# A gated mix of attention and MLP: the first attention turn put into the MLP's last token tile, and the MLP in text order

## The chip, the core and the metric

The kernel runs on one core of a Trainium2 chip. The time is the device time of one execution in microseconds (us); lower is better. The core's engines are named as the profile names them: PE (TensorE, matmuls; PEld is its weight load), DVE (VectorE), ACT (ScalarE), POOL (GpSimd) and SP (SyncE, which here only issues DMAs). PE writes into PSUM, which has eight banks of 128 x 512 fp32 numbers. The profile also shows the clock that PE was granted, 1.00 being full speed.

## The reference

x has 2048 tokens of 448 features, all in fp32:

```
a = attention(x)                 # 16 heads of 28: softmax(q k^T / sqrt(28)) v, then @ wo
b = gelu(layernorm(x) @ w1 + b1) @ w2 + b2      # 448 -> 1792 -> 448
g = sigmoid(sum(x * gate_w))     # one number for each token
out = g * a + (1 - g) * b
```

The kernel reaches fp32 accuracy by splitting each operand of the large products into a high and a low part (`..h`, `..l`) and adding three products: high x high, high x low, low x high. To split means a rounding copy on ACT and a subtraction on DVE or POOL. The 448 features lie in four rows of 128 partitions, of which the last holds high and low halves of the remaining 64, so a product over the features is 11 matmuls and not 12.

## The kernel before

**Stages.** Tokens go in four chunks c of 512, each of four token tiles of 128.

1. *Projections.* For each chunk seven `qk_tile` (11 matmuls each, L161) and four `v_tile` (L175), results stored to DRAM. Layer norm's statistics are made beside them: `ln_stats(i)` (L194) fetches two token tiles of x and takes batch-norm statistics and aggregates on DVE, `ln_rows` (L201) makes rows of mean and 1/std, and `ln_turn(a, b)` (L207) turns them so that they lie along the tokens: for mean and for 1/std a transpose on PE into one bank, a copy on DVE, a DMA to DRAM. The first turn stands in chunk 1, the second in chunk 3. `ln_load` (L105) fetches the rows of a chunk back, to all partitions; `ln_fetch` (L110) and `ln_apply` (L114) make the normed input y of a chunk.
2. *MLP.* For each chunk, `mlp1(f)` for 14 groups f of 128 hidden features (11 matmuls, L451; ACT makes gelu twice, rounded L454 and full L455; POOL makes the low part hl, L456), then `mlp2(c, i)` for four token tiles (14 x 3 matmuls, L463 to L466; ACT copies the result, L469; SP stores it to gbs, L470). In chunk 0 the weights are loaded and split on the way: `load_w1` (L87: DMA, ACT copy, POOL subtraction), three f ahead, and `load_w2` (L96: DMA, ACT copy, DVE subtraction), through a staging tile with three buffers.
3. *Attention.* Units of work are the 512 queries of one head against 128 keys. A turn takes U = 5 units: `scores` (L620) makes 15 products (L629) into banks 0 to 4, with the exponentials of three units in one ACT instruction and of two in another (L634); then `pv_mm` (L655) multiplies earlier turns' exponentials by v into bank 7. There are 205 turns.

**Fillers.** The exponentials need each query's largest score. `RowMax` (L262) gets these: a matmul of queries by keys (L321) into a bank, then a reduce on DVE (L301 one bank, L303 two banks at once). There are 1040 such pieces, 65 for each group of 4 heads and chunk of queries, the 65th being `close` (L285: a transpose, a negated copy, a DMA to `ms`). They fill in between other work: 476 of them (MLP_MAX) in the MLP, where `Filler.run` (L370) lets a group of six go into banks 2 to 7 each time that enough have come due over the slots of the MLP's matmuls; the others in attention, up to three for each turn, in banks 5, 6 and 5. `load_qm(n)` (L424) brings the maxima of a chunk of queries into the query tile, and before that forces whatever pieces are still missing for it, one by one through bank 5.

**Order.** PE takes its matmuls in the order of the program text in all stages. On the other engines the order of the projections and the MLP is worked out by a scheduler, that of attention is the text's. An engine with its order fixed can only do its next instruction: where that waits, all behind it wait too.

**Between the MLP and attention.** After mlp1 of chunk 3, the first keys, queries and values are fetched. Turn 0 follows the last token tile. At its start SP issues the loads of `khi(1)` and of b2 (`b2b`, L679), and for k = 2 to 5 `load_wo` (L590: DMA, then DVE's cast woh at L593, then POOL's subtraction). The gate's sigmoid (L611 to L614) stands ahead of turn 0. The last turns project the results (`finish`, `gated`, `finish_last`).

```
         for i in range(TPC):
             if c + 1 < NC:
                 ln_fetch(c + 1, i)
                 ln_apply(c + 1, i)
             mlp2(c, i)
```

## Time and profile before

| | |
|---|---|
| runs | 1151.25, 1142.76, 1155.83 us; median 1151.25 |
| profiled execution | 1146.98 us; span 1145.2 us, mean granted clock 0.991 |
| projections | 0 to 126.7 us of the span |
| MLP | 126.7 to 486.4 us |
| attention | 486.4 us to the end |
| DVE, largest group | reduces of row maxima (L301), 624 of 687 ns, 413.4 us |
| ACT, largest group | exponentials (L634), 410 of 1234 ns, 484.6 us |

The page gives for each engine its busy time, share of the span and number of instructions. Its second part cuts the span into 40 equal slices of 28.6 us, one digit each: the busy tenths, or for PEclk the granted clock in tenths. A timeline row gives start, duration, engine, line, operation, what is written and read, shape, and in brackets how long the engine was idle before it and what ended that.

### The profile page before, as it was taken

The page shows a single profiled execution, that of the slowest core. Times are in us where ns is not written, and L with a number is a line of the kernel's source. Part 1 is how long each engine was busy: PE and PEld are TensorE (multiplying, and loading weights), DVE is VectorE, ACT ScalarE, POOL GpSimd, SP SyncE. Part 2 cuts the span into 40 slices and gives each one's busy share as a digit, 9 for nine tenths or more (in the row PEclk, how much of TensorE's full clock was granted, in tenths as well). Part 3 has the DMA queues.
Part 4 walks back from the last instruction along what each step waited for, and adds up shares of the span by engine and source line. Part 5 has one row for each costly group of instructions (what it writes and reads, how often), then busy time and mean ns, then how long its engine had stood idle before and what let it go on. Part 6 is the DMA issues. An engine that isn't in the chain of part 4 may idle for free.

```text
span 1145.2 us, 19823 instructions
## 1 busy us (share of the span) xinstructions
PE 1116.6 (98%) x8136; PEld 678.4 (59%) x8136; DVE 731.6 (64%) x1033; ACT 635.9 (56%) x668; POOL 331.0 (29%) x355
## 2 busy tenths in 40 slices
PE   6999989999999999989999999999999999999998
PEld 4778867777767777744444444444444444454556
DVE  3433287888878888666676766676676667646103
ACT  5324551132033032067887878878787887848463
POOL 4043367146044032011123012311222123444250
PEclk9999999999999999989999999999999999999999
DMA  8878643002100014062101211111121003002201
GB/s 269 277 217 303 208 141 88 25 9 68 47 23 18 25 30 114 25 168 72 30 12 36 52 40 40 36 27 39 31 64 36 18 19 91 12 25 68 66 26 49
DMA packets 53519, 84.35 MB, mean 74 GB/s; under 512 B 8676, under 2 KB 28660, under 8 KB 52628
## 3 DMA queue, kind: packets, MB, share of 16 engines
q1 hardware_dynamic: 49236, 76.96, 22.5%
q0 software_dynamic: 4192, 6.12, 2.1%
q8 instruction: 64, 1.05, 0.4%
q14 instruction: 27, 0.22, 0.1%
HBM read 56.40 MB, written 26.49 MB: 72 GB/s over the span
## 4 chain that ended last, share of the span: by engine, by line
PE 89%; DMA 4%; POOL 3%; DVE 2%; issue 1%; ACT 1%; SPq 0%; POOLq 0%; ACTq 0%; DVEq 0%
PE bank L658 22%; PE bank L629 20%; PE bank L321 15%; PE bank L451 10%; PE bank L168 4%; PE bank L466 4%; PE bank L463 4%; PE bank L464 4%; PE bank L184 2%; PE bank L525 1%; DMA bxr<-in_xk 1%; PE bank L526 1%; PE bank L527 1%; DMA xraw<-in_xt 1%; POOL hl L456 1%
## 5 line engine op out<-in xcount | busy, mean ns | idle before, releaser
L634 ACT ACTIVATE pt<-bank 128x1536 f32<-128x1536 f32 (+1 forms) x410 | 484.6, 1234 | 155.9 <-PE bank L629 155.9
L301 DVE TENSOR_REDUCE mx<-bank 128x1 f32<-128x512 f32 x624 | 413.4, 687 | 174.9 <-PE bank L321 161.0
L658 PE MATMUL bank<-pt,vg 128*32 128x512 f32 x2048 | 263.7, 606 | 0.0
L303 DVE TENSOR_REDUCE mx<-bank 128x2 f32<-128x1024 f32 x200 | 235.4, 1219 | 41.1 <-PE bank L321 41.0
L321 PE MATMUL bank<-khi,qd 28*128 28x512 f32 x512 | 241.6, 479 | 0.3 <-DVE mx L301 0.2
L321 PEld LDWEIGHTS bank<-khi,qd 28*128 28x128 f32 x512 | 92.3, 181 | 148.3 <-DVE mx L301 107.0
L629 PE MATMUL bank<-qh,klo 28*128 28x512 f32 x1024 | 179.0, 395 | 0.0
L629 PE MATMUL bank<-qh,khi 29*128 29x512 f32 x768 | 161.8, 484 | 0.3 <-ACT h L469 0.3
L451 PE MATMUL bank<-y,w1f 128*128 128x512 f32 x616 | 153.2, 400 | 0.6 <-ACT h L455 0.6
L451 PEld LDWEIGHTS bank<-y,w1f 128*128 128x128 f32 x616 | 113.8, 190 | 36.1 <-issue 12.5
L629 PE MATMUL bank<-ql,khi 28*128 28x512 f32 x768 | 133.6, 393 | 0.0
L456 POOL TENSOR_TENSOR hl<-h,hh 128x512 fp32r<-128x512 f32 x56 | 72.5, 1295 | 172.0 <-ACT h L455 160.8
L658 PEld LDWEIGHTS bank<-pt,vg 128*32 128x32 f32 x2048 | 45.7, 108 | 84.6 <-issue 83.1
L629 PEld LDWEIGHTS bank<-qh,klo 28*128 28x128 f32 x1024 | 90.2, 186 | 4.2
L321 PE MATMUL bank<-khr,qd 28*128 28x512 f32 x512 | 80.7, 467 | 7.3 <-DVE mx L303 4.2
L541 POOL DMA_DIRECT2D lt<-ob x15 | 10.8, 723 | 265.7 <-DVE ob L540 265.7
L466 PE MATMUL bank<-w2h,hl 128*128 128x448 f32 x224 | 85.1, 380 | 1.9 <-POOL hl L456 1.9
L469 ACT ACTIVATE h<-bank 128x448 f32<-128x448 f32 x16 | 8.7, 543 | 140.4 <-PE bank L466 140.4
L629 PEld LDWEIGHTS bank<-qh,khi 29*128 29x128 f32 x768 | 63.3, 183 | 36.8 <-ACT pt L634 32.1
L463 PE MATMUL bank<-w2h,hh 128*128 128x448 f32 x224 | 84.7, 378 | 0.3 <-ACT hh L454 0.3
L454 ACT ACTIVATE hh<-bank,b1s 128x512 fp32r<-128x512 f32 x56 | 38.4, 685 | 81.9 <-PE bank L451 81.8
L464 PE MATMUL bank<-w2l,hh 128*128 128x448 f32 x224 | 82.3, 368 | 0.0
(100 smaller groups left out, 1237.0 us busy)
## 6 DMA issues: line engine op xcount, KB each, us to landing
qk<-hl SPq DMA_DIRECT2D x28, 512.0 KB
xraw<-in_xt SPq DMA_DIRECT2D x16, 256.0 KB
vs<-vt SPq DMA_DIRECT2D x16, 256.0 KB
r<-in_xt SPq DMA_DIRECT2D x16, 256.0 KB
rc<-rls POOLq DMA_DIRECT2D x60, 64.0 KB, 2.2
bxr<-in_xk SPq DMA_DIRECT2D x8, 448.0 KB
r<-in_w SPq DMA_DIRECT2D x14, 256.0 KB
gbs<-h SPq DMA_DIRECT2D x16, 224.0 KB
```

Source lines behind the costliest of these rows:

```text
L168: nc.tensor.matmul(ps, a, b, start=(i == 0), stop=(i == len(ops) - 1))
L301: nc.vector.reduce_max(self.mx[:, c0:c0 + 1], bank[:, b0], axis=AX)
L303: nc.vector.reduce_max(self.mx[:, c0:c1 + 1:c1 - c0], bank[:, b0:b1 + 1], axis=AX)
L321: nc.tensor.matmul(bank[:, b], self.qds[self.n][r, i * P:(i + 1) * P], khi[self.n // NC][r, k * 512:(k + 1) * 512], start=True, stop=True)
L451: nc.tensor.matmul(ps, a, b, start=(i == 0), stop=(i == len(ops) - 1))
L456: nc.gpsimd.tensor_sub(hl[f], h, hh[f].bitcast(F32))
L463: nc.tensor.matmul(a, hh[f][:, sl], w2h[f], start=(f == 0), stop=False)
L464: nc.tensor.matmul(a, hh[f][:, sl], w2l[f], start=False, stop=False)
L466: nc.tensor.matmul(a, hl[f][:, sl], w2h[f], start=False, stop=(f == NF - 1))
L629: nc.tensor.matmul(bank[:, u % U], a[r, k * P:(k + 1) * P], b[r], start=(i == 0), stop=(i == 2))
L634: nc.scalar.activation(t, bank[:, b:b + len(units)], AF.Exp, scale=SCALE)
L658: nc.tensor.matmul(pv[32 * j:32 * j + 32, :], vg[n // NC][:, k, 32 * j:32 * j + 32], probs.pop(4 * step + j), start=(k == 0), stop=(k == N ...
```

## The change

Three things are changed.

1. *Layer norm's statistics.* The fetch of x (`stats_fetch`) and its use (`ln_stats`) are two functions, called at different tiles, the use two tiles or so after the fetch. In `ln_turn` both transposes come first, and one copy moves both rows; the first turn is one tile later, and `ln_load(0)`, `ln_fetch(0, ..)` and `ln_apply(0, ..)` are moved with it.
2. *The MLP in text order* on SP, POOL, ACT and DVE too. Weights are fetched (`fetch_w1`, `fetch_w2`) and split (`split_w1`, `split_w2`) apart: in chunk 0, step f fetches w1 of f+3 and w2 of f, runs mlp1(f), then splits w1 of f+2 and w2 of f-1. Staging is two tiles used in turn, and during the weights' loading the two halves of `lnr` as well. A chunk's `ln_apply` comes behind the token tile's matmuls, not ahead of them.
3. *The first turn of attention* (units 0 to 4) stands within the last token tile's matmuls, after its group f = 4. That tile accumulates in bank 7 and takes no fillers, so 476 pieces are spread over 42 slots fewer. The turn's exponentials go into a tile each of `klo` and `vg`. The gate's operations come ahead of chunk 3's token tiles. In attention the loop skips `scores` for turn 0, and with it the call that asks how many fillers are due.

The diff, cut:

```diff
-    def staged(width):
-        return my.tile([P, CH], F32, name="r", bufs=3)[:, :width]
+    stages, turn = [my.tile([P, CH], F32, name=f"s{i}") for i in range(2)], 0
+
+    def staged(width=CH):
+        nonlocal turn
+        turn += 1
+        return stages[turn % len(stages)][:, :width]
...
+    def split_w1(f):
+        r = wraw.pop((1, f)).rearrange("p (t x) -> p t x", t=4)
         t = mw1.tile([P, 8, P], F32R, name=f"w1f{f}")
         w1h[f], w1l[f] = t[:, 0:4], t[:, 4:8]
-        r = r.rearrange("p (t x) -> p t x", t=4)
         nc.scalar.activation(w1h[f], r, AF.Copy)
         nc.gpsimd.tensor_sub(w1l[f], r, w1h[f].bitcast(F32))
...
+    def split_w2(f):
+        r = wraw.pop((2, f))
         nc.scalar.activation(w2h[f], r, AF.Copy)
         nc.vector.tensor_sub(w2l[f], r, w2h[f].bitcast(F32))
...
             for n in range(2):
-                r = qw.tile([b - a, P], F32, name=f"rows{a}{n}")
                 nc.tensor.transpose(ps[:b - a, n * P:(n + 1) * P], mr[:, n, a:b], ident)
-                nc.vector.tensor_copy(r, ps[:b - a, n * P:(n + 1) * P])
-                nc.sync.dma_start(lns[n * NT + a:n * NT + b], r)
+            r = qw.tile([b - a, 2, P], F32, name=f"rows{a}")
+            nc.vector.tensor_copy(r, ps[:b - a, :2 * P].rearrange("p (n i) -> p n i", n=2))
+            for n in range(2):
+                nc.sync.dma_start(lns[n * NT + a:n * NT + b], r[:, n])
...
-                if c == 1 and m == 1:
+                if c == 1 and m in (1, 2):
+                    ln_stats(m - 1)
+                if c == 1 and m == 3:
                     ln_rows(0, TPC)
-                if c == 1 and m == 5:
+                if c == 1 and m == 6:
                     ln_turn(0, TPC)
...
+                if c == 3 and m == 1:
+                    stages += [lnr[:, 0], lnr[:, 1]]
...
     def mlp2(c, i):
 
         sl = slice(i * P, (i + 1) * P)
-        a = bank[:, i % 2, :D]
+        last = c * TPC + i == NT - 1
+        a = bank[:, 7 if last else i % 2, :D]
...
-            filler.run(1)
+            if not last:
+                filler.run(1)
+            elif f == NF // 3:
+                scores(list(range(U)), 0, early)
...
+    with tc.manual_schedule(engines={E.SP, E.Pool, E.Activation, E.DVE}):
+        for c in range(NC):
+            for f in range(NF):
+                if c == 0:
+                    if f + 3 < NF:
+                        fetch_w1(f + 3)
+                    fetch_w2(f)
...
+                    if f == FS:
+                        filler.spread(nc.sync, MLP_MAX, (NC * NF - FS) * 23 - 3 * NF)
+                mlp1(f)
+                if c == 0:
+                    if f + 2 < NF:
+                        split_w1(f + 2)
+                    if f > 0:
+                        split_w2(f - 1)
...
+                nc.scalar.activation(gate, zall, AF.Exp, scale=-1.0)
...
+            for i in range(TPC):
+                mlp2(c, i)
+                if c + 1 < NC and i < 3:
+                    ln_apply(c + 1, i)
...
-            scores(units, min(3, filler.due()))
+            if u:
+                scores(units, min(3, filler.due()), lambda n: ap.tile([P, n, CH], F32, name=f"pt{n}"))
```

More of the change, by code (lines that the diff above doesn't have):

```diff
@@ L82, with fetch_w1, fetch_w2 @@
     w1h, w1l, w2h, w2l = {}, {}, {}, {}
-    def staged(width):
-        return my.tile([P, CH], F32, name="r", bufs=3)[:, :width]
-    def load_w1(f):
-        r = staged(CH)
-        nc.sync.dma_start(r, w1[f].rearrange("p t x -> p (t x)"))
+    stages, turn = [my.tile([P, CH], F32, name=f"s{i}") for i in range(2)], 0
[3 more added lines that the diff above has]
+        return stages[turn % len(stages)][:, :width]
+    wraw = {}
+    def fetch_w1(f):
+        wraw[1, f] = staged()
+        nc.sync.dma_start(wraw[1, f], w1[f].rearrange("p t x -> p (t x)"))
+    def split_w1(f):
+        r = wraw.pop((1, f)).rearrange("p (t x) -> p t x", t=4)
         t = mw1.tile([P, 8, P], F32R, name=f"w1f{f}")
         w1h[f], w1l[f] = t[:, 0:4], t[:, 4:8]
-        r = r.rearrange("p (t x) -> p t x", t=4)
         nc.scalar.activation(w1h[f], r, AF.Copy)
         nc.gpsimd.tensor_sub(w1l[f], r, w1h[f].bitcast(F32))
-    def load_w2(f):
-        r = staged(D)
-        nc.sync.dma_start(r, w2[f])
+    def fetch_w2(f):
+        wraw[2, f] = staged(D)
+        nc.sync.dma_start(wraw[2, f], w2[f])
+    def split_w2(f):
+        r = wraw.pop((2, f))
         nc.scalar.activation(w2h[f], r, AF.Copy)
@@ L110, in ln_fetch @@
     def ln_fetch(c, t):
-        lnx[c, t] = staged(CH)
+        lnx[c, t] = staged()
         nc.sync.dma_start(lnx[c, t], xt[t, :, c * CH:(c + 1) * CH])
@@ L192, with stats_fetch @@
         mr = qw.tile([P, 2, NT], F32, name="mr")
+        bxr = {}
+        def stats_fetch(i):
+            bxr[i] = qx.tile([P, 2, D], F32, name="bxr")
+            nc.sync.dma_start(bxr[i], xk[2 * i:2 * i + 2].rearrange("t p d -> p t d"))
         def ln_stats(i):
-            x = qx.tile([P, 2, D], F32, name="bxr")
-            nc.sync.dma_start(x, xk[2 * i:2 * i + 2].rearrange("t p d -> p t d"))
+            x = bxr.pop(i)
             for n in range(2):
@@ L237 @@
                 if c == 0 and m in (3, 5):
-                    ln_stats(m // 4)
-                if c == 1 and m == 1:
+                    stats_fetch(m // 4)
+                if c == 1 and m in (1, 2):
+                    ln_stats(m - 1)
+                if c == 1 and m == 3:
                     ln_rows(0, TPC)
-                if c == 1 and m == 5:
+                if c == 1 and m == 6:
                     ln_turn(0, TPC)
-                if c == 1 and m == 6:
-                    ln_load(0)
-                if c == 1 and m >= 4 or c == 2 and m < 3:
-                    ln_stats(m - 2 if c == 1 else m + 5)
-                if c == 2 and m in (0, 1, 2, 4):
-                    ln_fetch(0, (0, 1, 2, 2, 3)[m])
-                if c == 2 and 3 <= m < 6 or c == 3 and m == 0:
-                    ln_apply(0, m - 3 if c == 2 else 3)
+                if c == 1 and m >= 3 or c == 2 and m < 2:
+                    stats_fetch(m - 1 if c == 1 else m + 6)
+                if c == 1 and m >= 5 or c == 2 and m < 4:
+                    ln_stats(m - 3 if c == 1 else m + 4)
+                if c == 2 and m == 1:
+                    ln_load(0)
+                if c == 2 and m in (2, 3, 5, 6):
+                    ln_fetch(0, (2, 3, 5, 6).index(m))
+                if c == 2 and m in (4, 5) or c == 3 and m in (0, 1):
+                    ln_apply(0, m - 4 if c == 2 else m + 2)
                 if c == 2 and m == 6:
@@ L254 @@
                     ln_turn(TPC, NT)
-                if c == 3 and m < 3:
-                    load_w1(m)
+                if c == 3 and m == 1:
+                    stages += [lnr[:, 0], lnr[:, 1]]
+                if c == 3 and m in (1, 2, 4):
+                    fetch_w1(m // 2 if m < 4 else 2) if m > 1 else fetch_w1(0)
+                if c == 3 and m in (4, 5):
+                    split_w1(m - 4)
             for i in range(TPC):
@@ L357, in spread @@
         def spread(self, queue, upto, slots):
-            if self.max is None:
-                self.max = RowMax()
             self.max.queue = queue
@@ L429, in load_qm, with scores, product, exps @@
         nc.sync.dma_start(qs[n][0][DH:P:32].bitcast(F32), ms[g][:, c * CH:(c + 1) * CH])
+    U, UA = 5, 3
+    probs = {}
+    def scores(units, most, tiles):
+        def product(u, i):
+            n, k, j = u // 4 // NT, u // 4 % NT, u % 4
+            g, (qh, ql) = n // NC, qs[n]
+            a, b, r = ((khi[g], qh, DH + 1), (klo[g], qh, DH), (khi[g], ql, DH))[i]
+            r = slice(32 * j, 32 * j + r)
+            nc.tensor.matmul(bank[:, u % U], a[r, k * P:(k + 1) * P], b[r], start=(i == 0), stop=(i == 2))
+        def exps(units):
+            t = tiles(len(units))
+            b = units[0] % U
+            nc.scalar.activation(t, bank[:, b:b + len(units)], AF.Exp, scale=SCALE)
+            for i, u in enumerate(units):
+                probs[u] = t[:, i]
+        first, last = units[:UA], units[UA:]
+        if most > 0:
+            filler.max.issue(5, 1, [(first[0] + 3) % 4])
+        for i in range(3):
+            for u in first:
+                product(u, i)
+        exps(first)
+        for i in range(3):
+            for u in last:
+                product(u, i)
+            if i == 0 and most > 1:
+                filler.max.issue(6, 1, [(first[0] + 1) % 4, (first[0] + 2) % 4])
+        if last:
+            exps(last)
+        if most > 2:
+            filler.max.issue(5, 1, [(first[0] + 1) % 4, (first[0] + 2) % 4])
     ml = ExitStack()
@@ L464, in mlp2 @@
             nc.tensor.matmul(a, hh[f][:, sl], w2l[f], start=False, stop=False)
-            filler.run(2)
+            if not last:
+                filler.run(2)
             nc.tensor.matmul(a, hl[f][:, sl], w2h[f], start=False, stop=(f == NF - 1))
-            filler.run(1)
+            if not last:
+                filler.run(1)
+            elif f == NF // 3:
+                scores(list(range(U)), 0, early)
         gb = mh.tile([P, CH], F32, name="h", bufs=2)[:, :D]
@@ L470, in mlp2 @@
         nc.sync.dma_start(gbs[c * TPC + i], gb)
-    for c in range(NC):
-        for f in range(NF):
-            if c == 0 and f + 3 < NF:
-                load_w1(f + 3)
-            if c == 0 and f == 0:
-                for k in range(4):
-                    load_khr(0, k)
-            if c == 0 and f == FS:
-                filler.spread(nc.sync, MLP_MAX, (NC * NF - FS) * 23)
-            if c == 0:
-                load_w2(f)
-            mlp1(f)
-        if c == NC - 1:
-            m0.close()
-            aq = ctx.enter_context(tc.tile_pool(name="aq", bufs=1, side="right", reuse_waits="tile"))
-            load_khi(0)
-            load_klo(0)
-            load_q(0)
-            load_v(0)
-            load_qm(0)
-        else:
-            ln_load(c + 1)
-        for i in range(TPC):
-            if c + 1 < NC:
-                ln_fetch(c + 1, i)
-                ln_apply(c + 1, i)
-            mlp2(c, i)
+    E = mybir.EngineType
@@ new lines, with early @@
+    with tc.manual_schedule(engines={E.SP, E.Pool, E.Activation, E.DVE}):
[5 more added lines that the diff above has]
+                    fetch_w2(f)
+                    if f == 0:
+                        filler.max = RowMax()
+                    if f < 4:
+                        load_khr(0, f)
+                    if f == FS:
[6 more added lines that the diff above has]
+                        split_w2(f - 1)
+            if c == 0:
+                split_w2(NF - 1)
+                stages[2:] = []
+            if c == NC - 1:
+                m0.close()
+                aq = ctx.enter_context(tc.tile_pool(name="aq", bufs=1, side="right", reuse_waits="tile"))
+                first = {3: aq.tile([P, S], F32, name="klo", bufs=2), 2: aq.tile([P, NT, P], F32, name="vg", bufs=2)}
+                def early(n):
+                    t = first[n] if n == 3 else first[n].rearrange("p a b -> p (a b)")
+                    return t[:, :n * CH].rearrange("p (n c) -> p n c", c=CH)
+                nc.scalar.activation(gate, zall, AF.Exp, scale=-1.0)
+                nc.vector.tensor_scalar_add(gate, gate, 1.0)
+                nc.vector.reciprocal(gate, gate)
+                nc.vector.tensor_scalar(ngate, gate, -1.0, 1.0, op0=OP.mult, op1=OP.add)
+                load_khi(0)
+                load_klo(0)
+                load_q(0)
+                load_v(0)
+                load_qm(0)
+            else:
+                ln_load(c + 1)
+                ln_fetch(c + 1, 0)
+                ln_fetch(c + 1, 1)
+            for i in range(TPC):
+                mlp2(c, i)
+                if c + 1 < NC and i < 3:
+                    ln_apply(c + 1, i)
+                    if i < 2:
+                        ln_fetch(c + 1, i + 2)
+                    else:
+                        ln_apply(c + 1, 3)
@@ L505 @@
     ap = sb("ap", 4)
-    U, UA = 5, 3
     aw = sb("aw", 1)
@@ L608, in gate_acc @@
             nc.gpsimd.tensor_scalar(a, a, ngate[:, tt:tt + 1], None, op0=OP.mult)
-    tc.keep_in_program_order(nc.scalar.activation(gate, zall, AF.Exp, scale=-1.0))
-    nc.vector.tensor_scalar_add(gate, gate, 1.0)
-    nc.vector.reciprocal(gate, gate)
-    nc.vector.tensor_scalar(ngate, gate, -1.0, 1.0, op0=OP.mult, op1=OP.add)
     filler.spread(nc.gpsimd, NG * NC * 65, ((NG * NC - 2) * NT + LQ - 1) * 4 // U)
-    probs = {}
-    def scores(units, most):
-        def product(u, i):
-            n, k, j = u // 4 // NT, u // 4 % NT, u % 4
-            g, (qh, ql) = n // NC, qs[n]
-            a, b, r = ((khi[g], qh, DH + 1), (klo[g], qh, DH), (khi[g], ql, DH))[i]
-            r = slice(32 * j, 32 * j + r)
-            nc.tensor.matmul(bank[:, u % U], a[r, k * P:(k + 1) * P], b[r], start=(i == 0), stop=(i == 2))
-        def exps(units):
-            t = ap.tile([P, len(units), CH], F32, name=f"pt{len(units)}")
-            b = units[0] % U
-            nc.scalar.activation(t, bank[:, b:b + len(units)], AF.Exp, scale=SCALE)
-            for i, u in enumerate(units):
-                probs[u] = t[:, i]
-        first, last = units[:UA], units[UA:]
-        if most > 0:
-            filler.max.issue(5, 1, [(first[0] + 3) % 4])
-        for i in range(3):
-            for u in first:
-                product(u, i)
-        exps(first)
-        for i in range(3):
-            for u in last:
-                product(u, i)
-            if i == 0 and most > 1:
-                filler.max.issue(6, 1, [(first[0] + 1) % 4, (first[0] + 2) % 4])
-        if last:
-            exps(last)
-        if most > 2:
-            filler.max.issue(5, 1, [(first[0] + 1) % 4, (first[0] + 2) % 4])
     def pv_mm(step):
@@ L661 @@
     pv = bank[:, 7]
-    E = mybir.EngineType
     steps = NG * NC * NT
```

## The prediction

> **What bounds the kernel now.** I read the page's busy shares first, then its 40 slices, then windows of 5 us, then the timelines of PE, DVE and SP around each hole.

> ```profile
> PE 1116.6 (98%) x8136; PEld 678.4 (59%) x8136; DVE 731.6 (64%) x1033; ACT 635.9 (56%) x668; POOL 331.0 (29%) x355
> ...
> PE   6999989999999999989999999999999999999998
> ...
> PEclk9999999999999999989999999999999999999999
> ```

> TensorE sets the time: 1116.6 of the span's 1145.2 us busy, so 28.6 us idle, plus matmuls at a lower granted clock. The change removes no matmul, so it can only move the idle time and the slow stretches. Part of the idle lies at the start (slice 1), which the change leaves alone. The rest sits where slices read 8; the windows on such places:

> ```profile
> 55.00:60.00 5.00, 1.35 (x6) 0.88 (x5) 3.67 (x9) 1.00 (x2) 0.00 (x0) 0.85 0.87 326
> 60.00:65.00 5.00, 5.00 (x20) 4.26 (x19) 0.69 (x1) 0.60 (x1) 0.00 (x0) 0.81 0.61 203
> 145.00:150.00 5.00, 2.61 (x15) 1.49 (x14) 3.74 (x5) 3.40 (x7) 3.72 (x3) 1.00 0.50 157
> 490.00:495.00 5.00, 3.35 (x22) 1.64 (x26) 2.87 (x5) 3.31 (x4) 1.12 (x1) 0.70 0.59 181
> 495.00:500.00 5.00, 5.00 (x34) 2.10 (x26) 2.72 (x5) 2.24 (x2) 1.14 (x1) 0.50 0.51 158
> ```

> Each row gives the window, its length, then PE, weight-load, DVE, ACT and POOL busy time, the granted clock, DMA share and GB/s. Three places stand out, and the change touches each: the layer norm's turn (55 to 62), the first mlp pass (127 to 189), and the step from mlp to attention (486 to 502). All sums below are against the profiled execution, 1146.98 us (span 1145.2 plus 1.8 around it); the median shown, 1151.25, is 4.3 higher.

> **(a) The two transposes of the statistics.** In the PE timeline the second waits for a copy on DVE:

> ```profile
> 55.02 0.27 PE L212 MATMUL bank<-ident,mr 128*4 128x128 f32 x1
> 58.94 0.37 PE L212 MATMUL bank<-ident,mr 128*4 128x128 f32 x1 [3.65 <-DVE rows L213]
> ```

> That copy stood on DVE behind statistics whose input came late (BN stats at 57.35, after 0.98 of waiting for DMA). Now both transposes stand together with nothing between them, and one copy follows; nothing on PE needs it soon, since eight banks rotate. The 3.65 us go, and so should the slow clock behind them: the seven matmuls from 58.96 to 62.03 took 3.07 us, against 7 x 0.233 = 1.63 at the pace of the 15 matmuls in 3.68 and less at 0.205, so 1.4. The second turn (112.47, wait 0.37) gives about 0.4. **−5.5**; bounds 0 (the copy still holds a bank PE wants) and −6. The later place of the turn (one tile on) and of the statistics costs nothing on PE: the row is needed only at 126.69.

> **(b) The first mlp pass.** From 126.69 to the end of its first token tile at 189.1 it takes 62.4 us. The work in it is 154 matmuls x 0.238 (15 take 3.68 in the rows below, with small gaps included) = 36.6, 42 x 0.205 = 8.6, and ten groups of six row-maximum matmuls x 0.68 = 6.8, together 52.0. So 10.4 are lost: waits 0.59 (139.97, for ACT), and

> ```profile
> 148.53 0.50 PE L321 MATMUL bank<-khr,qd 28*128 28x512 f32 x2 [2.39 <-DVE mx L303]
> 148.96 3.68 PE L451 MATMUL bank<-y,w1f 128*128 128x512 f32 x15
> 159.12 0.50 PE L321 MATMUL bank<-khr,qd 28*128 28x512 f32 x2 [1.78 <-DVE mx L303]
> ...
> 185.44 0.47 PE L463 MATMUL bank<-w2h,hh 128*128 128x448 f32 x1 [0.34 <-ACT hh L454]
> ...
> 188.66 0.74 PE L466 MATMUL bank<-w2h,hl 128*128 128x448 f32 x1 [1.89 <-POOL hl L456]
> ```

> which are 7.0 with the 0.59; the rest is slow clock: 15 matmuls in 5.29 instead of 3.68 from 159.55 (granted clock 0.66), and about 1.5 from 188.7 on, with 0.3 in small gaps.

> With text order the weight splits stand at fixed places, and two chains set the pace. A step f on PE lasts 11 x 0.238 = 2.6 us and, with its share of the fillers, 3.1. (1) w1's low half for f+2 comes on POOL behind hl(f): hh 0.58, h 0.68, hl 1.25, w1l 1.29 and the hand-offs, 4.1 us after the end of step f, of which step f+1 covers 3.1. It binds on every second f: about 1.0 at f=2 and 4, and some 0.45 at 6, 8, 10, 12 where a filler group lies between: 3.7. (2) w2's subtraction on DVE waits for ACT's four operations (2.3) and takes 0.6 alone; with the three reduces of a group (3.5, two matmuls each at 1.2) that is 6.4 us against two steps' 6.2, so a group is late by little: 0.9 at every third group or so, 3.7 in all. What goes: the 1.89 before hl and its slow clock, since nothing of POOL's is behind at the end of the pass, and the two long reduce waits. 7.4 lost instead of 10.4: **−3.0**. No row shows this order, so bounds: −7 (the lost time down to the small waits), +12 (each group waits as at 148.53, below).

> **(c) From the last token tile to attention.** It now holds the 15 products of turn 0 and accumulates in bank 7. Before, turn 0 took 487.22 to 488.65 after the tile's end at 486.4, with its exponentials behind it, and fillers wait on DVE:

> ```profile
> 490.65 0.49 PE L321 MATMUL bank<-khr,qd 28*128 28x512 f32 x1 [2.00 <-DVE mx L301]
> ...
> 493.47 0.79 PE L321 MATMUL bank<-khr,qd 28*128 28x512 f32 x1 [1.01 <-DVE mx L301]
> ```

> The second of these is turn 1's last, 7.07 us after the tile's end. Why it comes then is on DVE and SP:

> ```profile
> 492.42 0.40 DVE L593 CAST woh<-ob 128x448 fp32r<-128x448 f32 x1 [1.83 <-DMA ob<-in_wo]
> 492.73 1.28 DVE L301 TENSOR_REDUCE mx<-bank 128x1 f32<-128x512 f32 x2
> ...
> 487.62 0.37 SPq L679 DMA_DIRECT2D b2b<-in_b  x1
> 488.05 0.44 SPq L592 DMA_DIRECT2D ob<-in_wo  x1
> ```

> The reduce that frees the bank stands behind the cast of wo's first group, which waits for a DMA issued at 488.05 that landed 4.28 us later; it is issued behind b2b, whose region is freed by the tile's last matmul and behind the tile's own store. This chain starts at the tile's end and is unchanged. The tile's end comes later by the products in it, 1.43 plus two switches of about 0.15 between shapes, so 1.7 to 1.9. Then turn 1 begins at once, is through in about 1.5 us and PE stands some 5 us for the same cast: its last filler comes at the new end plus 7.07. The turn won is thus lost again: **+1.9**. The slow clock after it (0.50 in 495 to 500, 0.77 in the next window) is paid both times. Bounds: −7.5 (the cast is not late; R1) and +3 (the longer stand costs more clock). The gate's operations, moved ahead of the tiles, hide under PE's 45.5 us of the four token tiles. If that cover went, it would be the 1.03 us that DVE waited for them at 488.73.

> [...]

> **(d) Denser fillers.** The same 476 row maxima are spread over 1154 slots, not 1196, since the last tile takes none: 3.6% denser. In mlp2, four tiles take 45.5 against 4 x 8.6 without fillers + 11.5 groups x 0.74 = 42.9; 2.6 are stalls of PE on DVE's reduces, over the three passes 7.8. DVE has 39.6 of 45.5 busy, the tightest place for it. DVE's load there, 39.6 of 45.5 or 0.87, becomes 0.90, and if stalls grow as one over what is left (0.13 to 0.10), 7.8 grows by 0.3 of itself: 2.3, of which the tile before the last, with fewer fillers, gives a little back: **+2.0**; bounds 0 and +4 (stalls half as long again).

> **(e) One turn fewer for the fillers of attention.** Turn 0 no longer asks for fillers: 187 turns for 564, three at most in each, and 564/188 is exactly three. So three are left for the forced loop ahead of the last query load, one by one through bank 5. The nearest row is the last maximum and close today, 0.58 of waiting at 1058.19. Two round trips of 0.5 + 0.69 + a hand-off of about 0.1, then final reduce and transpose 0.5, less 0.86 that today's close costs: **+2.2**; bounds 0 (PE has the projection of 2.6 us beside it) and +3.5.

> **Sum**: −5.5 − 3.0 + 1.9 + 2.0 + 2.2 = −2.4, so 1144.6, **1145 us**, −0.2%. With (b) at half its span either way and (c) to (e) at their ends the forecast's own range is 1138 to 1152. Within 1% is what a measurement of this kernel can't tell from no change.

> **R1, faster: the step to attention closes.** If the wo load is on time (its issue no longer behind the store and b2b), turn 1 has no 5 us hole and, with no hole, no clock of 0.50. Before, turn 5's exponentials came 22.3 us after the tile's end; at 2.92 a turn with nothing late they come at about 14.8. That is −7.5 in place of +1.9: 1135.2. For it: DVE has nothing else to do there once the gate is gone. Against: the chain store, b2b, DMA, cast hangs on the tile's last matmul alone. It carries with it the case that (b) does better than −3. Chance 0.25.

> **R2, slower: the split of w2 blocks the row maxima.** In text order a subtraction that waits for ACT holds every reduce behind it on DVE, and PE holds for the banks. If each of the eight groups of the pass waits 2.39 as at 148.53, that is 19.1, with POOL's 3.7 as above 22.8 against 10.4: +12.4 in place of −3.0, so 1160.0. It decides where the chain of 6.4 passes two steps of 6.2; it does by 0.2 on my numbers, so a 10% longer hand-off is enough to make it regular. Against: each late group also makes PE late, which gives DVE the time back. Chance 0.17.

> **R3: the transposes don't part from DVE.** If the copy of rows still holds PE, (a) is 0 and the time 1150.1. Chance 0.08; the forecast has 0.50.

> **How the numbers follow.** R1 is over 1% faster (1135.2 against 1135.5), R2 over 1% slower (1158.5): faster 0.25, within 1% 0.58, slower 0.17. The range reaches a little past R1 and nearly to R2: 1133 to 1157.

> **What would show it.** (a): no wait at the second transpose, clock 1.00 from 55 to 65. (b): pass and first tile take 59.4; POOL's w1l named at f=2 and 4. (c): a PE hole of about 5 us just after the last tile, ended by the reduce behind woh. (d): more of PE's waits on mx in mlp2. (e): two waits of about 1 us before the last turn's scores. I am wrong if DVE's order makes the first pass regularly late, or if the hole in (c) isn't there.

## The result and the profile after

The changed kernel takes 1155.42 us (median of 20 runs, 1148.42 to 1160.71), the kernel before 1148.30 (20 runs, 1141.60 to 1155.83). The ratio is 1.0067, 95% interval 1.0051 to 1.0082: **0.67% slower**, some 7.7 us by the ratio (7.1 between the medians), where 0.2% faster was forecast. That is near the upper end of the stated range (1133 to 1157) and within 1%, but the sign is wrong. The profiled execution shown here took 1159.02 us (span 1157.2); it is one of the longer runs, so its stages show what happened and where, and the sizes are taken from several kernels' profiles below.

The page of the changed kernel, busy shares and the same slices as before:

```profile
PE 1127.3 (97%) x8136; PEld 681.4 (59%) x8136; DVE 734.4 (63%) x1031; ACT 634.7 (55%) x668; POOL 334.2 (29%) x355
...
PE   6999999999999999979999999999999999999998
```

Busy time of PE went up, from 1116.6 to 1127.3 us, with the same 8136 matmuls; idle time went from 28.6 to 29.9. A part of the busy time is a lower clock: 25.5 us of it lie in stretches at 0.50, 18.6 before, which is some 3.4 us of the 10.7. The rest is matmuls that follow each other more slowly without a gap that the page counts as idle, as in tiles 1 to 11, where PE counts as busy but for 0.5 us. The 8 at slice 6, which holds most of the first mlp pass, is a 9 now, and at slice 18, the step to attention, the 8 has become a 7. The windows of the forecast, on the changed kernel (window, length, busy time of PE, weight load, DVE, ACT and POOL, granted clock, DMA share, GB/s):

```profile
55.00:60.00 5.00, 5.00 (x25) 4.03 (x24) 1.89 (x3) 2.24 (x4) 0.00 (x0) 1.00 0.99 349
60.00:65.00 5.00, 5.00 (x26) 4.60 (x25) 3.64 (x10) 2.21 (x4) 0.00 (x0) 1.00 0.98 341
145.00:150.00 5.00, 4.37 (x22) 2.94 (x22) 5.00 (x5) 3.41 (x7) 3.27 (x3) 1.00 0.39 119
490.00:495.00 5.00, 3.06 (x25) 2.08 (x23) 0.00 (x0) 2.91 (x3) 0.00 (x0) 1.00 0.32 77
495.00:500.00 5.00, 1.13 (x5) 0.48 (x9) 1.90 (x4) 0.00 (x0) 1.70 (x2) 0.76 0.71 194
```

The hole at 55 us is closed: PE is busy throughout at clock 1.00. At 145 PE gains, but DVE is now busy for all 5.00 us. At 495 PE stands for nearly four of five us. Two more places are new. PE's timeline at the first, at the hole of 495 and at the second:

```profile
448.05 0.50 PE L346 MATMUL bank<-khr,qd 28*128 28x512 f32 x2 [0.84 <-DVE mx L328]
449.18 0.50 PE L346 MATMUL bank<-khr,qd 28*128 28x512 f32 x2 [0.63 <-DVE mx L328]
450.31 0.80 PE L346 MATMUL bank<-khr,qd 28*128 28x512 f32 x2 [0.63 <-DVE mx L328]
...
498.87 0.79 PE L346 MATMUL bank<-khr,qd 28*128 28x512 f32 x1 [5.81 <-DMA ql<-qk]
...
1069.14 0.50 PE L346 MATMUL bank<-khi,qd 28*128 28x512 f32 x1 [0.95 <-DVE mx L326]
1070.68 0.28 PE L312 MATMUL bank<-ident,mf 128*16 128x128 f32 x1 [1.04 <-DVE mf L362]
```

The first three stand in tile 12, the first token tile of chunk 3, where nothing was forecast. The hole of 5.81 is the one that (c) forecast, and the last two are those of (e). What the waits cost is more than their sum, because of the clock behind them:

```profile
445.00:450.00 5.00, 3.21 (x15) 2.07 (x14) 3.74 (x6) 1.15 (x2) 1.00 (x1) 0.98 0.90 192
450.00:455.00 5.00, 4.69 (x13) 3.83 (x14) 3.65 (x4) 0.00 (x0) 0.00 (x0) 0.50 0.63 143
...
1065.00:1070.00 5.00, 3.69 (x18) 2.54 (x14) 1.60 (x4) 0.83 (x1) 4.80 (x5) 1.00 0.12 45
1070.00:1075.00 5.00, 4.32 (x24) 2.31 (x28) 0.87 (x3) 2.37 (x2) 1.79 (x2) 0.60 0.03 8
```

The granted clock is 0.50 behind the first group of waits and 0.60 behind the second. Tile 12 took 17.0 us instead of 11.3.

Why tile 12's reduces were late stands on DVE and ACT (start, length, engine, line):

```profile
443.96 0.68 ACT L516 ACTIVATE h<-bank,b1s 128x512 f32<-128x512 f32 x1
444.65 1.28 ACT L572 ACT_TABLE_LOAD   x1
445.95 0.21 ACT L572 ACTIVATE gate<-zall 128x16 f32<-128x16 f32 x1
...
446.19 0.17 DVE L573 TENSOR_SCALAR gate<-gate 128x16 f32<-128x16 f32 x1 [2.96 <-ACT gate L572]
...
446.78 6.87 DVE L328 TENSOR_REDUCE mx<-bank 128x2 f32<-128x1024 f32 x6
```

The gate's exponential stands on ACT behind the last gelu of chunk 3 and a table load. DVE's first gate instruction comes after 2.96 us of idle time that ended with it, and six maxima that PE wrote at 443.66 wait behind that instruction. When the reduces start at 446.78, the next group of six is due, and PE waits for its banks.

Since one profile is one execution, the stages of all profiled kernels side by side, in us, cut at the same instructions (the first is from the last matmul of chunk 0's projections to the first of the MLP; the third to the first matmul of tile 12; the fourth from there to DVE's copy of attention's first result; the last is the last full chunk of queries). The experiments' edits follow below.

| kernel | rest of projections | first mlp pass + tile 0 | tile 1 to tile 11 and mlp1 | tile 12 to first result | last full chunk |
|---|---|---|---|---|---|
| before | 86.9 | 62.7 | 254.8 | 89.7 | 47.1 |
| before, turn together | 80.9 | 65.3 | 253.8 | 89.8 | 47.1 |
| before, wo casts later | 83.4 | 64.1 | 254.0 | 88.0 | 47.1 |
| before, turn together and wo casts later | 81.1 | 62.5 | 255.3 | 86.6 | 47.1 |
| changed | 80.5 | 62.4 | 258.2 | 96.2 | 52.6 |
| changed, gate later | 80.8 | 65.9 | 258.0 | 92.9 | 52.6 |
| changed, wo casts later | 84.6 | 64.3 | 258.4 | 85.9 | 52.6 |
| changed, 479 maxima in the MLP | 81.0 | 64.7 | 259.3 | 92.9 | 47.0 |
| changed, splits first | 80.8 | 61.7 | 258.2 | 91.1 | 52.6 |
| changed, 1184 slots | 80.8 | 64.2 | 255.5 | 93.6 | 52.6 |
| changed, no maxima in the first pass | 81.6 | 60.0 | 266.6 | 95.6 | 52.6 |
| all five, 479 maxima | 80.8 | 63.8 | 256.0 | 83.7 | 47.1 |
| all five, 478 maxima | 80.8 | 64.2 | 255.4 | 85.3 | 46.3 |
| improved, without the early turn | 80.8 | 61.4 | 253.9 | 93.2 | 47.1 |

Column five repeats within 0.1 us for the same code and the same number of maxima, column three within 1.5. The first repeats within 1.1 but for the two kernels with only the casts of wo later: in the changed one PE once waited 2.07 us for a split of x on DVE, and in the one before the wait for the turn's copy was 1.60 instead of 3.65, with the clock at 1.00 behind it. The second and fourth differ by several us, and the dips of the clock with them: of two kernels with the same first pass the one with the gate later has a clock of 0.71 from 160 to 165 us and 0.95 in the next window, and takes 65.9, while the changed one has 1.00 in every window from 140 to 175, and takes 62.4.

### The profile page after: what moved, and what is told of

Read it like the earlier page. It is cut to its first block, busy times and chain, and to the rows that moved or that the text cites. A ratio compares the mean times of both kernels' runs of the same rounds, so it can differ in the third digit from the quotient of the medians.

```text
span 1157.2 us, 19820 instructions
## 1 busy us (share of the span) xinstructions
PE 1127.3 (97%) x8136; PEld 681.4 (59%) x8136; DVE 734.4 (63%) x1031; ACT 634.7 (55%) x668; POOL 334.2 (29%) x355
## 4 chain that ended last, share of the span: by engine, by line
PE 89%; DVE 4%; DMA 2%; issue 2%; POOL 1%; ACT 1%; SPq 0%; DVEq 0%; POOLq 0%
PE bank L708 21%; PE bank L466 20%; PE bank L346 15%; PE bank L512 10%; PE bank L179 6%; PE bank L529 4%; PE bank L525 4%; PE bank L526 4%; DVE mx L328 3%; PE bank L195 2%; PE bank L618 1%; PE bank L619 1%; PE bank L620 1%; DMA lt<-ob 1%; DMA wraw<-in_wqk 0%
## 5 line engine op out<-in xcount | busy, mean ns | idle before, releaser
L466 PE MATMUL bank<-qh,klo 28*128 28x512 f32 x1024 | 180.0, 397 | 0.0
L466 PE MATMUL bank<-qh,khi 29*128 29x512 f32 x768 | 162.1, 484 | 0.0
L512 PEld LDWEIGHTS bank<-y,w1f 128*128 128x128 f32 x616 | 112.2, 188 | 39.9 <-issue 11.3
L466 PE MATMUL bank<-ql,khi 28*128 28x512 f32 x768 | 134.4, 394 | 0.0
L346 PE MATMUL bank<-khr,qd 28*128 28x512 f32 x512 | 86.5, 473 | 10.7 <-DMA ql<-qk 5.8
L708 PEld LDWEIGHTS bank<-pt,vg 128*32 128x32 f32 x2038 | 45.7, 108 | 84.6 <-issue 83.7
L466 PEld LDWEIGHTS bank<-qh,klo 28*128 28x128 f32 x1024 | 91.0, 187 | 4.3
L466 PEld LDWEIGHTS bank<-qh,khi 29*128 29x128 f32 x768 | 63.4, 183 | 36.0 <-ACT pt L471 31.8
## 6 DMA issues: line engine op xcount, KB each, us to landing
xraw<-in_xt SPq DMA_DIRECT2D x16, 256.0 KB
vs<-vt SPq DMA_DIRECT2D x16, 256.0 KB
s<-in_xt SPq DMA_DIRECT2D x16, 256.0 KB
```

The source lines that it names most:

```text
L346: nc.tensor.matmul(bank[:, b], self.qds[self.n][r, i * P:(i + 1) * P], khi[self.n // NC][r, k * 512:(k + 1) * 512], start=True, stop=True)
L466: nc.tensor.matmul(bank[:, u % U], a[r, k * P:(k + 1) * P], b[r], start=(i == 0), stop=(i == 2))
L512: nc.tensor.matmul(ps, a, b, start=(i == 0), stop=(i == len(ops) - 1))
L708: nc.tensor.matmul(pv[32 * j:32 * j + 32, :], vg[n // NC][:, k, 32 * j:32 * j + 32], probs.pop(4 * step + j), start=(k == 0), stop=(k == N ...
```

## The experiments

Ratios are to the kernel before, run on the same chip; the changed kernel's is 1.0067.

**The turn of the statistics alone**, on the kernel before:

```diff
             for n in range(2):
-                r = qw.tile([b - a, P], F32, name=f"rows{a}{n}")
                 nc.tensor.transpose(ps[:b - a, n * P:(n + 1) * P], mr[:, n, a:b], ident)
-                nc.vector.tensor_copy(r, ps[:b - a, n * P:(n + 1) * P])
-                nc.sync.dma_start(lns[n * NT + a:n * NT + b], r)
+            r = qw.tile([b - a, 2, P], F32, name=f"rows{a}")
+            nc.vector.tensor_copy(r, ps[:b - a, :2 * P].rearrange("p (n i) -> p n i", n=2))
+            for n in range(2):
+                nc.sync.dma_start(lns[n * NT + a:n * NT + b], r[:, n])
```

> The kernel before, with one edit: both transposes of the statistics' turn stand together and one copy moves both rows. Theory: the 3.65 us wait at 58.94 and the slow clock after it go, 5 to 6.5 us faster than before, ratio 0.9945 to 0.9955. Rival: the gain seen in the changed kernel is due to the statistics being fetched earlier; then the wait stays in part and the ratio is over 0.997.

Measured 1143.66 against 1148.99, ratio 0.9952 (0.9932 to 0.9973), 5.5 us faster. Windows of this kernel:

```profile
55.00:60.00 5.00, 5.00 (x25) 4.09 (x24) 3.75 (x9) 2.32 (x4) 0.00 (x0) 1.00 1.00 367
60.00:65.00 5.00, 5.00 (x27) 4.58 (x26) 0.72 (x2) 1.09 (x2) 0.00 (x0) 1.00 0.79 240
```

No wait and no slow clock, with the statistics fetched where they always were. (a) is this edit alone, and its size was right. The rival, that the earlier fetch of the statistics does it, is excluded. The rest of the change therefore costs 1.0067 − 0.9952, 1.15% or 13 us.

**The gate's operations later:**

```diff
-                nc.scalar.activation(gate, zall, AF.Exp, scale=-1.0)
...
             for i in range(TPC):
+                if c == NC - 1 and i == TPC - 1:
+                    nc.scalar.activation(gate, zall, AF.Exp, scale=-1.0)
...
                 mlp2(c, i)
```

> The changed kernel, with the gate's four operations (exponential on ACT, three on DVE) moved from ahead of chunk 3's first token tile to ahead of its last. Theory: in the changed kernel they hold DVE for 2.96 us at 443 to 446 while a group of six row maxima waits behind them, PE then waits 0.84, 0.63 and 0.63 for banks and falls to a granted clock of 0.50; that first tile takes 17.0 us instead of 11.3. So: tile 12 back to 11.3 to 12, no clock below 1.00 from 440 to 465, time 5 to 6 us below the changed kernel, ratio to the kernel before near 1.002. Rival: that tile is late because of the denser row maxima; then the tile stays above 15 us and the time within 2 us of the changed kernel, ratio near 1.006.

Measured 1154.37, ratio 1.0041 (1.0021 to 1.0062): 3.0 us below the changed kernel. Windows where the changed kernel had its dip:

```profile
445.00:450.00 5.00, 5.00 (x28) 3.89 (x26) 4.03 (x5) 1.50 (x3) 2.57 (x2) 1.00 0.86 195
450.00:455.00 5.00, 4.90 (x29) 3.41 (x27) 4.26 (x4) 0.00 (x0) 0.00 (x0) 1.00 0.87 184
```

Tile 12 takes 11.6 us and the clock stays at 1.00, as the theory said; the gain in the median is smaller than the 5 to 6 expected, because the profile's 17.0 was a bad case: with the gate unmoved and all the rest of tile 12 the same, the kernels with wo casts later and with the splits first have it at 14.2 and 14.1. The profile shows the mechanism; the two kernels' ratios overlap in their intervals, so the medians alone do not settle its size.

**The casts of wo later:**

```diff
-                    if 2 <= k < 6:
-                        load_wo(k - 2)
+                    if 4 <= k < 8:
+                        load_wo(k - 4)
+                    if 2 <= k < 6:
+                        fetch_wo(k - 2)
```

`fetch_wo` issues the DMA alone, and `load_wo` casts and subtracts.

> The changed kernel, with each cast of wo on DVE (and its subtraction on POOL) two steps later than its fetch, the fetches left where they are. Theory: the hole of 5.81 us on PE after the last token tile is the first cast, which waits for its DMA with turn 1's reduces behind it. So: no PE wait over 1 us there, no clock of 0.50 in the 10 us after, time 6 to 10 us below the changed kernel, ratio 0.998 to 1.002. Rival: the hole is from the DMA traffic or the query loads that the releaser names (DMA ql); then the wait stays over 4 us and the ratio near 1.006.

Measured 1150.94, ratio 1.0018 (0.9999 to 1.0037), 5.6 us below the changed kernel, a little under the 6 to 10 expected. DVE and PE, first of the changed kernel:

```profile
497.82 0.39 DVE L686 CAST woh<-ob 128x448 fp32r<-128x448 f32 x1 [23.88 <-DMA ob<-in_wo]
498.13 1.28 DVE L326 TENSOR_REDUCE mx<-bank 128x1 f32<-128x512 f32 x2
```

then of this one:

```profile
494.66 2.01 DVE L326 TENSOR_REDUCE mx<-bank 128x1 f32<-128x512 f32 x3 [17.73 <-PE bank L346]
...
500.72 0.39 DVE L691 CAST woh<-ob 128x448 fp32r<-128x448 f32 x1 [1.31 <-DMA ob<-in_wo]
...
501.77 0.50 PE L346 MATMUL bank<-khr,qd 28*128 28x512 f32 x1 [0.55 <-DVE mx L326]
506.05 0.50 PE L346 MATMUL bank<-khr,qd 28*128 28x512 f32 x1 [1.20 <-DVE mx L326]
```

The cast was the hole: turn 1's reduces no longer stand behind it, and the wait of 5.81 is gone, with waits of 0.55 and 1.20 left and the clock at 1.00 in every window from 490 to 510. The releaser named on PE's row, DMA ql, was not it; the reduce that ended at 498.82, behind the cast, was.

**The same on the kernel before:**

> The kernel before, with the casts of wo two steps later than their fetches. Theory: the cast of wo holds the step to attention in the kernel before as well; its waits of 2.00 and 1.01 us shrink and the clock of 0.50 after them goes in part: 2 to 6 us faster, ratio 0.995 to 0.998. Rival: there the gate's operations on DVE hold the first reduce, so the time moves by less than 1.5 us, ratio 0.999 to 1.001.

Measured 1145.86 against 1147.34, ratio 0.9985 (0.9968 to 1.0003): 1.7 us, not told apart from nothing by its interval. In its profile the wait of 1.01 is gone from where it stood, but that of 2.00 is still there (1.99), the one behind the gate's operations. The rival holds in part: before, the gate and the cast each held one reduce.

**Maxima counted so that none is forced:** MLP_MAX 479 instead of 476, and two slots fewer in attention's spread.

> The changed kernel, with 479 instead of 476 row maxima in the MLP and the others spread over two slots fewer, so that none is left for the forced loop ahead of the last chunk of queries. Theory: the three forced ones cost two waits of 0.95 and 1.04 us and a clock of 0.66 behind them, 5.5 us in the profiled run. So: no wait there, time 3 to 5.5 below the changed kernel, ratio 1.002 to 1.004. Rival: the loss there is the projection's or chance, not the forced pieces; then ratio near 1.006.

Measured 1154.76, ratio 1.0045 (1.0024 to 1.0066). The last full chunk takes 47.0 us instead of 52.6, so the waits and the dip behind them cost 5.5 us and are gone. The median gives back only 2.5 us (the intervals of the two ratios overlap), since a new loss came at the very end. Windows of the end:

```profile
1146.00:1148.00 2.00, 1.63 (x9) 1.16 (x7) 2.00 (x4) 0.00 (x0) 0.00 (x0) 1.00 0.29 109
1148.00:1150.00 2.00, 0.00 (x0) 0.00 (x0) 0.35 (x1) 0.00 (x0) 0.00 (x0) 0.95 0.94 350
1150.00:1152.00 2.00, 0.00 (x0) 0.00 (x0) 0.00 (x0) 0.00 (x0) 0.00 (x0) 0.50 0.00 0
1152.00:1154.00 2.00, 0.00 (x0) 0.00 (x0) 0.00 (x0) 0.00 (x0) 0.00 (x0) 0.50 0.00 0
1154.00:1157.00 3.00, 0.00 (x0) 0.00 (x0) 0.00 (x0) 0.00 (x0) 0.00 (x0) 0.50 0.00 0
```

From 1150 on no engine works and no DMA moves, and the span ends at 1157.0. After DVE's last instruction the changed kernel goes on for 2.9 us, this one for 8.7.

**Fewer maxima per slot:** 476 over 1184 slots instead of 1154.

> The changed kernel, with the 476 row maxima of the MLP spread over 1184 slots instead of 1154, so that they reach to 18 slots before the end of the last tile but one. Theory: the denser spread costs 2.7 us in chunks 1 and 2 and more in chunk 3; most of it returns, 2 to 3.5 us, ratio 1.0035 to 1.005. Rival: PE's loss there does not depend on the density; ratio near 1.0065, or above, if the last pieces hold bank 7 for the last tile.

Measured 1148.72, ratio 1.0018 (0.9998 to 1.0037), 5.6 us below the changed kernel, more than expected. Tiles 1 to 11 give 2.7, of which about 0.7 is one group of six maxima that now stands behind them. Tile 12 takes 10.5 us, with two groups instead of three: with another spacing a group of reduces fills the time until the exponential is done, and the gate's first instruction on DVE comes at 445.66 without idle time ahead of it. The kernel with 479 missed them for the most part (a wait of 1.14 on DVE, one of 0.63 on PE, tile 12 at 12.6). So the single gains of gate, count and slots hold the same loss and must not be added.

**Splits ahead of mlp1(f):** the block of `split_w1(f + 2)` and `split_w2(f - 1)` moved ahead of `mlp1(f)`.

> The changed kernel, with both weight splits of a step (w1 of f+2, w2 of f-1) ahead of mlp1(f) in the text, not behind it. Theory: in the changed kernel's first mlp pass PE waits for POOL's w1 low half (2.6 us in all, up to 1.01 each) because that stands behind gelu and hl of f, and for reduces behind w2's subtraction; with the splits first these chains start a step earlier. So: no wait on POOL w1f, first mlp pass 46 to 48 us instead of 49.0, ratio 1.003 to 1.006. Rival: the pass is set by something else (the low half's own time or DVE's load); then the pass stays at 48.5 to 49.5 and the ratio near 1.006. A worse outcome is possible if a split waits for its weights' DMA and holds the gelu behind it.

Measured 1152.00 against 1147.34, ratio 1.0066 (1.0037 to 1.0095): no gain. The pass with its tile takes 61.7 against 62.4, inside what repeats scatter. PE's waits for POOL's w1f are gone, and three for reduces (0.88, 0.63, 0.63 at 139.8 to 142.1) stand in their place. The rival holds: two things bind the pass, one just behind the other.

**No maxima in the first pass:** FS = 13, 476 over 1085 slots.

> The changed kernel, with the row maxima of the MLP starting at f = 13 of chunk 0 instead of f = 4 (476 over 1085 slots, so denser later). Theory: the first mlp pass of 49.0 us is held by DVE, which has per group of fillers three reduces (3.5 us) and 1.3 subtractions of w2 (0.6 to 1.7 us each) against 4.1 us of PE; without fillers the pass is 154 matmuls of 0.238 = 36.7 plus 2 to 4 us of waits for POOL's w1 low half, 38 to 41. Rival: the chain of ACT and POOL holds it; then the pass stays above 43.

Measured in one run 1162.53, and the pass takes 46.1 us (121.74 to 167.80): the theory of DVE alone falls. PE and POOL:

```profile
142.20 2.79 PE L512 MATMUL bank<-y,w1f 128*128 128x512 f32 x11 [0.63 <-POOL w1f L102]
145.47 2.79 PE L512 MATMUL bank<-y,w1f 128*128 128x512 f32 x11 [0.47 <-POOL w1f L102]
148.89 2.81 PE L512 MATMUL bank<-y,w1f 128*128 128x512 f32 x11 [0.63 <-POOL w1f L102]
...
140.88 1.27 POOL L102 TENSOR_TENSOR w1f<-lnr,w1f 128x512 fp32r<-128x512 f32 x1
142.50 1.30 POOL L517 TENSOR_TENSOR hl<-h,hh 128x512 fp32r<-128x512 f32 x1 [0.35 <-ACT h L516]
143.75 1.66 POOL L102 TENSOR_TENSOR w1f<-s,w1f 128x512 fp32r<-128x512 f32 x1
...
141.08 1.55 DVE L111 TENSOR_TENSOR w2l<-lnr,w2h 128x448 fp32r<-128x448 f32 x1 [3.50 <-ACT w2h L110]
143.44 0.84 DVE L111 TENSOR_TENSOR w2l<-s,w2h 128x448 fp32r<-128x448 f32 x1 [0.81 <-ACT w2h L110]
```

With no fillers, from 142 us on every step of 11 matmuls ends in a wait for w1's low half, at about 3.3 us a step. That is chain (1) of the forecast: 4.1 after the end of a step plus 2.6 for a step of matmuls, for two steps. With the fillers DVE comes in beside it.

**All five edits**, and the same with 478 maxima:

> The changed kernel with all five edits of the other experiments on it (gate later, wo casts later, count of 479, splits first, 1184 slots). Theory: the four losses (gate 5.5, wo 6, forced pieces 4, density 2.5) add up and the turn of the statistics keeps its gain, so 14 to 20 us below the changed kernel, ratio 0.989 to 0.995 to the kernel before. If the losses overlap (one clock dip shared), ratio 0.995 to 1.000.

Measured 1145.14, ratio 0.9988 (0.9973 to 1.0003). By the stages the gains add up as expected, to PE's end at 1133.97 (1153.58 in the changed kernel), but the tail of 8.7 us is there as in the other kernel with 479.

> As the kernel with all five edits, but with 478 row maxima in the MLP instead of 479, so that the load of the next chunk's queries stays on POOL's queue and one piece is left for the forced loop. In the two kernels with 479 the span went on for 8.7 us after the last DVE instruction, with no engine and no DMA busy in the last 7; in the others it is 2.9. Theory: this tail hangs on where that load is issued; then it is 2.9 again and the time 5 us below the all-edits kernel, ratio 0.992 to 0.995. Rival: the tail comes with another count, or from the order of the end itself; then the ratio stays near 0.999.

Measured 1138.53 (6 runs) against 1147.40, ratio **0.9911** (0.9881 to 0.9941): faster than both kernels, and the tail is 2.9 again. Page lines:

```profile
PE 1115.1 (98%) x8136; PEld 677.6 (60%) x8136; DVE 735.8 (65%) x1030; ACT 635.0 (56%) x668; POOL 333.8 (29%) x355
...
PEclk9999999999999999999999999999999999999999
```

**The kernel before with turn and wo edits only**, and **the improved kernel without the early turn**:

> The kernel before with two edits alone: both transposes of the statistics together, and the casts of wo two steps later. Theory: both gains of the single runs (0.9952 and 0.9985) add: ratio 0.993 to 0.995. If the all-edits kernel with 478 isn't faster than this one, text order and the early turn bring nothing of their own. Rival: text order and the early turn are worth several us once their side costs are gone; then this is slower by 3 us or more than that kernel.

> The changed kernel with the gate later, the wo casts later and the splits first, and with turn 0 put back behind the last token tile (476 maxima over 1196 slots, 188 turns asked for fillers, as before). Theory: with the hole closed the early turn is worth something, since its exponentials are done when turn 1 begins: this kernel is 2 to 6 us slower than the one with 478 and the early turn. Rival: the early turn only moves 15 matmuls; then the two are within 1.5 us.

Measured 1143.05, ratio 0.9956 (0.9934 to 0.9979), a little short of the 0.993 to 0.995 expected, and 1142.79, ratio 0.9959 (0.9935 to 0.9983). These two differ in text order, in when the statistics are fetched, in the gate's place and in the splits, and come out the same: no gain of text order is seen here. The kernel with the early turn and its side costs removed is 4.3 us faster than the latter, by medians; but the intervals overlap, and the two also differ by two maxima and in their spacing. That the early turn is worth something is likely, and its size is not settled.

## Why the prediction was wrong

**(a) −5.5.** Right, in mechanism and size: −5.5 by the edit alone, with the interval from −7.8 to −3.1. That it fits to the tenth is luck, since the wait and the clock behind it differ between two profiles of the same code (86.9 and 83.4 in the table).

**(b) −3.0.** Not there. Over the profiles of the kernel before and its three variants pass and tile 0 take 62.5 to 65.3, mean 63.7; over the five with the changed order in this pass 62.4 to 65.9, mean 64.3. The step that failed is "what goes ... the two long reduce waits". Chain (1) binds at about its size (waits for POOL of 2.6 us where 3.7 was forecast), but chain (2) left out that the split of w1 on POOL and that of w2 on DVE, set side by side in the text, overlap and then take longer: POOL's up to 1.77 us, 1.27 at its shortest, and DVE's up to 1.71 instead of the 0.6 that I took. DVE in the changed kernel:

```profile
141.34 3.48 DVE L328 TENSOR_REDUCE mx<-bank 128x2 f32<-128x1024 f32 x3
144.74 1.67 DVE L111 TENSOR_TENSOR w2l<-s,w2h 128x448 fp32r<-128x448 f32 x1
146.33 3.47 DVE L328 TENSOR_REDUCE mx<-bank 128x2 f32<-128x1024 f32 x3
```

DVE then has 5 us of work for this group of fillers, with no idle time, and PE 4.1 (14.5 slots of 0.238 and the group's 0.66), so the long waits came back as short ones, of up to 0.63. No run parts the two splits from each other, so this cause of (b) is argued from the rows. The working also counted about 1.5 us of slow clock behind 188.7 as a loss of a pass that ended at 189.1; most of it lies behind that end. R2's mechanism (w2's split and the reduces in one line on DVE) is at work, at a price far below the 12.4 it was given: late groups slow PE too, as its counter-argument said.

**(c) +1.9.** The hole was forecast by place, cause and size: a third filler 7.07 us after the tile's end, measured 7.55 (491.32 to 498.87), behind the cast. It hid the turn won. The last tile's products took 1.6 us (484.13 to 485.73), so with the 0.48 by which the hole ends later (c) measured about +2.1. The slow clock behind it was paid both times at the same price: turn 5's exponentials came 15.27 us after that filler, before 15.23. The clock stood at 0.50 for 10.24 us in both (492.02 to 502.26 before, 497.58 to 507.82 now), so the longer stand of 5.81 cost no more clock than the waits before, and the case behind the bound of +3 did not come. (The clock of 0.50 before began at 492.02, behind the wait of 2.00 alone; that of 1.01 came when it had already fallen.) R1's mechanism is what the later casts do; it is not what the change does.

**The gate's operations, at nothing.** This is the step that failed outright: "hide under PE's 45.5 us of the four token tiles". They need little time, but in text order DVE meets the first of them while ACT is still behind the last gelu. The cover that counted was not PE's work but that of DVE's own line: what stood behind the waiting instruction was a group of six maxima. The price, named as 1.03 if the cover went, was a wait of 2.96, three waits of PE and a clock of 0.50: 3.0 us by the ratios, up to 5.7 in a profile.

**(d) +2.0.** Right in sign and about in size. Tiles 1 to 11 with their mlp1 passes went from a mean of 254.5 to 258.2, +3.7; but they hold 378 maxima now instead of 366, two groups more, and tile 14 none instead of 20 (it takes 8.7 us instead of 12.1). Two groups at the forecast's 0.74 are 1.5 us that have only moved, so some 2.2 are the closer spacing's. The size is in part luck: the working took 45.5 us for four tiles, and those of chunk 1 take 44.2 (266.77 to 310.98), which halves, in its own sum, the stalls that it let grow. Nor did the change need the closer spacing. Before, the 1196 slots ended 48 short of the MLP's 1244, and the last maximum came at 475.91, ahead of the last tile at 477.70; without the last tile's 42 there are still 1202. Besides, the closer spacing set a group where the gate stood.

**(e) +2.2.** The two waits came as forecast, 0.95 and 1.04. The term left out is the clock behind them, 0.60 from 1070 to 1075; the last full chunk costs 5.5 more, not 2.2. An estimate from the trace: 6.8 us at 0.50 (1071.02 to 1077.85) cost 3.4 us of work at full clock, and with the waits 5.4.

The sum with the measured terms: −5.5 + 0.6 + 2.1 + 3.0 + 2.2 + 5.5 = +7.9, against +7.7 by the ratio; the terms are taken from different runs, and (b) and the gate scatter by 3 us from one profile to the next, so that it closes this well is luck. No single rival came true. The forecast failed because two of its terms, gate and (e), priced a wait without the slow clock behind it, and because (b)'s gain was counted from the waits that the old order had, without the load that the new one makes. Its own range of 1138 to 1152 does not follow from its terms either: with (b) at half its span and (c) to (e) at their ends it would be about 1129 to 1156.

## What to carry to other kernels

In a fixed order, ask of every instruction that waits what stands behind it in its own engine's line, not only whether the bound engine has work meanwhile; a few small operations put ahead of a busy stretch can hold a whole group of buffers (here the gate's held six banks, with DVE idle for 2.96 us). Price a wait of PE with the slow clock behind it, and count several waits of under 1 us close together too (here 0.84, 0.63 and 0.63, with 6.83 us at 0.50 behind them). When part of a stage loses its fillers, count where they go before calling the longer stage a loss. Moving work earlier pays only when what it waited beside (here the cast behind a DMA) goes as well, and edits tested singly may remove the same loss, so test the sum too.

## What the runs showed of the hardware

```profile
446.38:449.79 3.41, 1.83 (x9) 0.79 (x7) 3.35 (x5) 0.00 (x0) 0.00 (x0) 1.00 0.91 197
449.79:453.20 3.41, 2.89 (x8) 2.24 (x9) 3.41 (x4) 0.00 (x0) 0.00 (x0) 0.50 0.86 186
453.20:456.62 3.42, 3.42 (x11) 2.85 (x9) 0.45 (x1) 0.00 (x0) 0.00 (x0) 0.50 0.64 191
456.62:460.03 3.41, 3.41 (x21) 2.67 (x20) 2.64 (x4) 0.00 (x0) 0.00 (x0) 1.00 0.57 144
...
143.86:147.28 3.42, 2.27 (x13) 1.37 (x11) 2.16 (x4) 1.64 (x3) 1.90 (x2) 1.00 0.53 177
147.28:150.69 3.41, 2.17 (x10) 1.64 (x11) 3.41 (x5) 2.58 (x6) 2.51 (x2) 1.00 0.66 195
```

The changed kernel's waits leave PE busy for 1.83 us of one step, and the next two run at 0.50. The wait of 2.39 (146.14 to 148.53) is shared out between two steps, with 2.27 and 2.17 of busy time, and neither brings the clock down. In these two profiles the steps at full clock that were followed by 0.50 had 0.00 to 1.83 us of PE's busy time, and none with 2.15 or more was. In the improved kernel a wait of 2.09 (138.45 to 140.54) was followed by three pairs of matmuls at 0.50 us each, to 143.30, where such a pair took 0.80 with the clock at 0.50 (450.31 in the changed kernel); the 15 matmuls from 143.23 on then took 5.31 instead of 3.73.

**Of overlapping subtractions on POOL and DVE the later one takes longer.** In the kernel with no maxima in the first pass DVE's took 1.55 us where POOL's had begun 0.20 earlier (141.08 and 140.88), and POOL's 1.66 instead of 1.27 where DVE's had begun 0.31 earlier (143.75 and 143.44). The later one ended 0.48 and 1.13 us after the other, a little less than the 0.62 that DVE's took at 140.80 in the changed kernel and the 1.27 of POOL's at 140.88 here. What holds the later one up is not shown.

**A tail at the program's end.** Both kernels with 479 maxima ended 8.7 us after DVE's last instruction, all others 2.9 to 3.0. By the kernel's text, with 479 one load of queries moves from POOL's DMA queue to SP's; with 478 it stays, and the tail measured 2.9. Why that queue should matter at the end is not shown.
